# Streaming V as the wide operand of the second-layer attention fill tiles, with the sums picked out of a bf16 high and a bf16 low part

## The chip, the cores and the metric

The kernel runs on one core of a Trainium2 chip. The metric is the device time of one launch in microseconds (us), the median of repeated runs. Three runs of the kernel before gave 316.36, 313.03 and 316.22 us, median 316.22 us.

## The reference

Four decode elements (one query token each, batch B = 4) go through the same two layers twice: grouped-query attention over a cache, then a GEGLU feed-forward block. Both attention passes read the same K and V caches and the same weights.

```python
def _A_ref(x, k_cache, v_cache, wq, wo):          # 32 query heads, 8 KV heads, Sk = 4096, Dh = 128
    q = (x @ wq).reshape(B, 1, 32, 128).transpose(0, 2, 1, 3)
    k = jnp.repeat(k_cache, 4, axis=1)
    v = jnp.repeat(v_cache, 4, axis=1)
    p = softmax(einsum("bhqd,bhkd->bhqk", q, k) * 128 ** -0.5)
    o = einsum("bhqk,bhkd->bhqd", p, v)
    return o.transpose(0, 2, 1, 3).reshape(B, 1, 4096) @ wo
def _B_ref(x, w_gate, w_up, w_down):              # D = 512, F = 1792
    return (gelu(x @ w_gate) * (x @ w_up)) @ w_down
x = x + A(layernorm(x)); x = x + B(layernorm(x))
x = x + A(layernorm(x)); x = x + B(layernorm(x))
```

All inputs are bf16. The K and the V cache have 16.8 million elements each.

## The kernel before, in words

**Tiles.** For one element, K and V are 8 KV heads x 2 halves (`t` = 0, 1) = 16 tiles each of 128 partitions x 16 rows x 128 columns (512 KB). K tiles of one element stay in 16 fixed buffers (`KT`); V tiles go through a ring of 7 buffers (`VRing`, `V_SLOTS = 7`). All DMAs are issued on SyncE (SP) in program order: `Keys.load` (L318) for K, `VRing.pump` (L423) for V. `pump` issues the next V tile of a fixed sequence as soon as a ring buffer is free; a buffer is free when the last matmul that reads it is done.

**Order of the elements.** The order of instructions is written out by hand (`tc.manual_schedule()`); each engine works through its own list in that order. Layer 1 of element b and layer 2 of element b-1 share one load of K and V as far as buffers allow. `attend(b)` first scores layer 2 of element b-1 against the K tiles that are still there (`scores`, L336), and each K tile that is done with is reloaded for element b. Then V arrives: first 16 tiles for layer 1 of b (the last 3 of these are kept in their buffers for layer 2), then 8 tiles, `other2`, which layer 2 of element b-1 needs again, then 5 tiles `own1` for layer 2 of element b. After layer 1's last tile the output projection ends (`OutProj`, L204), and `dense` runs the feed-forward block of element b: `add_x`, `stats`, the gate matmuls `g`, the up matmuls `u`, the down matmuls `y`. Then the main loop (from L714) makes the second layer's query and calls `attend(b+1)`.

**Values.** `Values.step` (L442) takes one V tile: 16 matmuls at L457, each with a 128x128 piece of V as the stationary operand (a weight load) and the 4 probability columns of the head as the moving one, summed into `ot`. When both tiles of two heads are done, VectorE multiplies `ot` by the reciprocal of the softmax sum (L479). `fill(n)` takes n tiles and leaves that multiply for `flush`.

**Where the 8 `other2` tiles stand.** They are filled into the feed-forward block and the query of the next layer, where no other V tile is used, for b = 1, 2 and 3. In the order of TensorE (PE) these places are, with the tiles taken there:

| place | where | before | after |
|---|---|---|---|
| P1 | `dense`, after `add_x`, ahead of `stats` | tile 1 | unit 1 |
| P2 | `dense`, after `g`, ahead of `u` | tile 2 | unit 2 |
| P3 | `dense`, after `u`, ahead of `down` | tile 3 | units 3, 4 |
| P4 | loop, after `add_x`, ahead of `stats` and `q_proj` | tile 4 | unit 5 |
| P5 | loop, after `q_proj`, ahead of `q_build` | tiles 5, 6 | unit 6, turn of pair 1 |
| P6 | loop, after `q_build`, ahead of `attend` | tiles 7, 8 | units 7, 8 |
| P7 | `attend`, after the scores of the first half | - | turn of pair 2 |

Three buffers of the ring hold the kept tiles at this time, so four circulate: tile 5 is issued when tile 1 is done with, and so on; `own1` follows tile 8.

**Softmax.** `soft` (L341 to L360), `soft_turn` (L363) and `soft_swap` (L378) make the probabilities `pe`, 128 partitions x (4 heads x 32 x 4) bf16, by way of PSUM tile `x` (one buffer) and a copy on ScalarE (ACT).

Of the kernel before, what the change touches and what calls it, by code (L numbers as in the profile page):

```python
# [31 lines left out]
def kernel(  # L32
# [35 lines left out]
    wts = ctx.enter_context(tc.tile_pool(name="wts", bufs=1))  # L68
    state = ctx.enter_context(tc.tile_pool(name="state", bufs=1))
    tmpp = ctx.enter_context(tc.tile_pool(name="tmpp", bufs=1))  # L70
    pep = ctx.enter_context(tc.tile_pool(name="pep", bufs=3))
    grp = ctx.enter_context(tc.tile_pool(name="grp", bufs=2))
    zp = ctx.enter_context(tc.tile_pool(name="zp", bufs=2 * NG))
    small = ctx.enter_context(tc.tile_pool(name="small", bufs=1))
# [29 lines left out]
    ident_bf = const.tile([P, P], BF16, name="ident_bf")  # L104
    mean_f = const.tile([P, P], FP32, name="mean_f")
    sel_bf = const.tile([P, BE, QD, QS], BF16, name="sel_bf")
    amask = const.tile([P, QD], FP32, name="amask")
    hmask = const.tile([P, rep], FP32, name="hmask")
    dmask = const.tile([P, GH, rep], FP32, name="dmask")
# [27 lines left out]
    def build_consts():  # L137
        nc.scalar.preload_act_table_set("natural_log_exp_and_others")
        nc.vector.memset(mean_f[:], 1.0 / D)
        nc.vector.memset(qb[:], 0.0)  # L140
        nc.vector.memset(xb[:, :, B:B + 1], 1.0 / D)
        nc.vector.tensor_reduce(out=amask[:], in_=ident_bf[:].rearrange("p (a i) -> p a i", a=QD),
                                axis=AX.X, op=ALU.max)
        iv = ident_bf[:].rearrange("p (b w e) -> p b e w", b=NB, e=2)
        for be in range(BE):
            nc.vector.tensor_copy(out=sel_bf[:, be],
                                  in_=iv[:, be // 2, be % 2].unsqueeze(1)
                                  .broadcast_to([P, QD, QS]))
        nc.vector.tensor_reduce(out=hmask[:], in_=ident_bf[:].rearrange("p (y h) -> p h y", h=rep),
                                axis=AX.X, op=ALU.max)  # L150
        nc.vector.scalar_tensor_tensor(
            out=dmask[:], in0=amask[:].unsqueeze(2).broadcast_to([P, GH, rep]), scalar=float(D),
            in1=hmask[:].unsqueeze(1).broadcast_to([P, GH, rep]), op0=ALU.mult, op1=ALU.mult)
# [12 lines left out]
    def ln_scale(nb, st):  # L166
        ss, mean = st[:, :, 0], st[:, :, 1]
        msq = small.tile([P, nb], FP32, name="msq", tag="msq")
        if nb == 1:
            nc.vector.tensor_scalar(out=msq[:], in0=mean, scalar1=mean, scalar2=LN_EPS,  # L170
                                    op0=ALU.mult, op1=ALU.subtract)
        else:
            nc.vector.tensor_copy(out=msq[:], in_=mean)
            nc.vector.tensor_tensor(out=msq[:], in0=mean, in1=msq[:], op=ALU.mult)
            nc.vector.tensor_scalar(out=msq[:], in0=msq[:], scalar1=LN_EPS, scalar2=None,
                                    op0=ALU.subtract)
        var = small.tile([P, nb], FP32, name="var", tag="var")
# [5 lines left out]
        mr = small.tile([P, nb], FP32, name="mr", tag="mr")  # L183
# [156 lines left out]
    def soft(sc):  # L340
        m = grp.tile([P, 1], FP32, name="m", tag="m", bufs=1)  # L341
        nc.vector.tensor_reduce(out=m[:], in_=sc.rearrange("p c j -> p (c j)"), axis=AX.X,  # L342
                                op=ALU.max)
        mt = grp.tile([P, QS], FP32, name="mt", tag="mt", bufs=1)
        nc.vector.transpose(out=mt[:], in_=m[:].broadcast_to([P, QS]))
        gm = grp.tile([P, rep], FP32, name="gm", tag="gm", bufs=1)
        nc.vector.tensor_reduce(out=gm[:], in_=mt.rearrange("p (y h) -> p h y", h=rep), axis=AX.X,
                                op=ALU.max)
        nm = grp.tile([P, 1], FP32, name="nm", tag="nm")
        junk = grp.tile([P, rep], FP32, name="junk", tag="junk", bufs=1)  # L350
        nc.vector.scalar_tensor_tensor(out=junk[:], in0=gm[:], scalar=-scale, in1=hmask[:],  # L351
                                       op0=ALU.mult, op1=ALU.mult, accum_out=nm[:])
# [20 lines left out]
        nc.vector.reciprocal(out=rden[:], in_=den[:])  # L373
        return rden

    def soft_swap(p0):
        pp = p0[0]
        x = ps_x.tile([P, GH, NT, CH, rep], FP32, name="x", tag="x")  # L378
        pT = pp.rearrange("p c (t a h) -> p a t c h", t=NT, a=QD)
        for s in range(GH):  # L380
            for a in range(QD):
                nc.tensor.matmul(x[a * QS:(a + 1) * QS, s], lhsT=ident_bf[:, s * QS:(s + 1) * QS],  # L382
                                 rhs=pT[:, a], start=True, stop=True, skip_group_check=True)
        pe = pep.tile([P, GH, C, rep], BF16, name="pe", tag="pe")
        nc.scalar.copy(out=pe.rearrange("p s c h -> p (s c h)"),  # L385
                       in_=x.rearrange("p s t c h -> p (s t c h)"))
        return pe
# [96 lines left out]
            return len(self.tiles) - self.n  # L484


    def dst1(k, n):
        return OT_bf[:, k * rep:(k + n) * rep]

# [73 lines left out]
        ring.extend(2, b, own)  # L563
        return proj.y

    def attend(b, qy):

        gx, gy = second_groups[b - 1]
        prob1, prob2 = {}, {}
# [1 line left out]
        turn = keys.turn  # L571
        kept2, own2, other2 = two(b - 1)
        kept1, own1, _ = two(b)
        vals2 = Values(2, b - 1, kept2 + own2 + other2, prob2, dst2(b - 1))
        vals1 = Values(1, b, one(b), prob1, dst1, keeps=kept1)

        sc2 = [new_scores() for g in range(NG)]
        for t in range(NT):
            scores(sc2[0], gx, t)
            keys.load(GH)  # L580
        p0 = soft(sc2[0])
        q_build(qy())
        soft_turn(p0)
# [13 lines left out]
        vals2.step(4)  # L597
        turn()
        vals2.step(3)
        pe1, den1 = soft_swap(p1), soft_den(p1)  # L600
        turn()
        prob2[gy] = (pe1, soft_recip(den1))
        sc1 = new_scores()
# [10 lines left out]
        q_build(q1_bf[:, gy, :, b])  # L614
        turn()
        vals2.step(len(kept2 + own2) - vals2.n)
        vals1.step(2)
        sc1 = new_scores()
        scores(sc1, gy, 0)
# [16 lines left out]
        vals1.step(1)  # L636
        proj.heads(heads[3] + rep, rep)
        assert vals1.left() == 0
        return proj.y, vals2

    def attend_last(qy):
        b = B - 1
        gx, gy = second_groups[b]
        prob2 = {}
        kept2, own2, other2 = two(b)
        vals = Values(2, b, kept2 + own2 + other2, prob2, dst2(b))
        ring.extend(2, b, other2)
        sc2 = [new_scores() for g in range(NG)]
        for t in range(NT):
            scores(sc2[0], gx, t)  # L650
            ring.pump([KT[gx * GH + s][t] for s in range(GH)])
# [10 lines left out]
        prob2[gy] = (soft_swap(p1), soft_recip(soft_den(p1)))  # L662
# [12 lines left out]
        return proj.y  # L675

    def dense(b0, nb, y, prev):
# [18 lines left out]
        prev.fill(1)  # L696
        u = sums(1, ffn_in(rhs, n, wu_sb, "u"))
        H_bf = gate_up(nb, sq, u, shifts(nb, mr, 1), rstd)
        prev.flush()
        prev.fill(1)  # L700
        return down(nb, H_bf)

    class NoValues:
        def fill(self, n):
            pass

        def flush(self):
            pass
# [5 lines left out]
    for b in range(B):  # L714
# [11 lines left out]
        nc.vector.tensor_scalar(out=tq[:], in0=cs_q[:], scalar1=mr[:, 0:1], scalar2=None,  # L726
                                op0=ALU.mult)
        qx = q_round(q, gx, rstd, tq)
        prev.flush()
        prev.fill(2)  # L730
        q_build(qx)
        prev.flush()
        prev.fill(TG)
        prev.flush()

        def qy(b=b, g=gy, rstd=rstd, tq=tq):
            return q_round(q_proj(lambda k: xb[:, k, b:b + 1], 1, g), g, rstd, tq)

        if b < B - 1:
            y, prev = attend(b + 1, qy)  # L740
        else:
            y = attend_last(qy)

    add_x(0, B, dense(0, B, y, NoValues()))
    xo_ps = ps_sm.tile([P, D], BF16, name="xo_ps", tag="sm")
# [35 lines left out]
```

## Time and profile before

| | |
|---|---|
| median of 3 runs | 316.22 us (313.03 to 316.36) |
| the profiled execution's own time | 315.57 us |
| its span, first to last instruction | 313.8 us |
| outside the span | 1.8 us |
| PE busy | 208.7 us, 66%, 5104 matmuls |
| DVE (VectorE) / ACT busy | 145.1 us, 46% / 32.9 us, 10% |
| DMA | 106.90 MB, mean 341 GB/s |
| chain that ended last | DMA 56%, PE 26%, DVE 7% |

The span is cut from the first to the last instruction of the program. PE is matmuls, PEld the weight loads that run beside them. In a timeline line the columns are start, duration, engine, source line, operation, out<-in by the program's names, shape, and the count of merged instructions; in brackets stands the idle time before the first of them and what ended it ("issue" means that the profile shows nothing that the engine waited for). "SPq" is SyncE's DMA queue. In the chain the columns are start, duration and what it was.

### The profile page before, as it was taken

What the parts mean: (1) busy time and instruction counts of PE and PEld (TensorE: products, weight loads), DVE (VectorE), ACT (ScalarE), POOL (GpSimd) and SP (SyncE); (2) the same over time, 40 slices, a digit from 0 to 9 for tenths busy, and PEclk for the clock granted to TensorE, in tenths of its full rate; (3) what the DMA queues carried; (4) which work ended last, traced back from release to release, by engine and by line L of the source; (5) the groups of instructions that cost most, each with busy time, mean ns of one, the idle gap of its engine ahead of it and who ended that gap; (6) DMA issues with size and microseconds to landing.
All of it is one profiled execution on the core that took longest, in us unless ns stands there. A gap on an engine that the chain in (4) does not pass through costs nothing.

```text
span 313.8 us, 11113 instructions
## 1 busy us (share of the span) xinstructions
PE 208.7 (66%) x5104; PEld 153.9 (49%) x5104; DVE 145.1 (46%) x372; ACT 32.9 (10%) x90; POOL 0.7 (0%) x6
## 2 busy tenths in 40 slices
PE   1464275324787667887838387788583778878893
PEld 0213145324546145786425247685261468845893
DVE  3576812012267894032378961322689731313333
ACT  2002002000012112000110202000022020002200
POOL 0000000000000000000000000000000000000000
PEclk9999999999999999999875655555557555555555
DMA  7999999999179999978999999968999999779800
GB/s 255 384 417 421 421 416 395 376 407 399 34 263 401 417 419 418 415 290 239 350 418 416 421 386 344 364 218 260 413 416 421 415 418 392 240 256 359 321 7 3
DMA packets 33503, 106.90 MB, mean 341 GB/s; under 512 B 2984, under 2 KB 8880, under 8 KB 33456
## 3 DMA queue, kind: packets, MB, share of 16 engines
q1 hardware_dynamic: 33456, 106.19, 88.3%
q8 instruction: 40, 0.66, 0.8%
q14 instruction: 7, 0.06, 0.1%
HBM read 106.17 MB, written 0.00 MB: 338 GB/s over the span
## 4 chain that ended last, share of the span: by engine, by line
DMA 56%; PE 26%; DVE 7%; SPq 5%; issue 4%; ACT 2%; ACTq 0%
DMA v_t<-in_A_v_cache_dram 27%; DMA kt<-in_A_k_cache_dram 23%; PE sc L336 7%; PE ot L457 6%; DMA wd_sb<-in_B_w_down_dram 5%; PE y L204 5%; PE q L204 2%; SPq L130 2%; ACT pp L355 2%; PE g L204 1%; PE u L204 1%; DVE m L342 1%; PE x L382 1%; SPq L131 1%; DVE pp L363 1%
## 5 line engine op out<-in xcount | busy, mean ns | idle before, releaser
L457 PE MATMUL ot<-pe,v_t 128*128 128x4 bf16 x1904 | 62.5, 167 | 29.0 <-DMA v_t<-in_A_v_cache_dram 19.9
L325 DVE STREAM_TRANSPOSE kt<-kt 128x1024 f32<-128x1024 f32 x64 | 75.1, 1214 | 6.5 <-DMA kt<-in_A_k_cache_dram 6.3
L457 PEld LDWEIGHTS <-v_t 128*128 128x128 bf16 x1904 | 58.5, 105 | 39.0 <-DMA v_t<-in_A_v_cache_dram 22.4
L336 PE MATMUL sc<-kt,qb 128*32 128x512 bf16 x512 | 62.9, 608 | 10.3 <-DVE kt L325 7.8
L336 PEld LDWEIGHTS <-qb 128*32 128x32 bf16 x512 | 17.3, 128 | 39.8 <-issue 32.1
L479 DVE TENSOR_TENSOR OT_bf<-ot,rden 128x8 bf16<-128x8 f32 (+1 forms) x40 | 6.5, 163 | 52.2 <-PE ot L457 52.1
L204 PE MATMUL y<-OT_bf,wo_sb 128*128 128x1 bf16 (+1 forms) x640 | 20.5, 165 | 9.4 <-DMA wo_sb<-in_A_wo_dram 7.7
L355 ACT ACTIVATE pp<-sc,nm 128x512 bf16<-128x512 f32 x16 | 11.0, 687 | 148.7 <-DVE junk L351 148.7
L204 PEld LDWEIGHTS <-wo_sb 128*128 128x128 bf16 x640 | 19.8, 105 | 10.0 <-DMA wo_sb<-in_A_wo_dram 8.1
L204 PE MATMUL q<-xb,wq_sb 128*128 128x1 bf16 (+1 forms) x640 | 18.5, 165 | 7.2 <-DMA wq_sb<-in_A_wq_dram 7.2
L204 PEld LDWEIGHTS <-wq_sb 128*128 128x128 bf16 x640 | 17.8, 103 | 11.2 <-DMA wq_sb<-in_A_wq_dram 8.2
L342 DVE TENSOR_REDUCE m<-sc 128x1 f32<-128x512 f32 x16 | 10.9, 682 | 25.2 <-PE sc L336 25.1
L382 PE MATMUL x<-pp,ident_bf 128*32 128x128 bf16 x256 | 9.7, 297 | 17.3 <-DVE pp L363 17.3
L382 PEld LDWEIGHTS <-ident_bf 128*32 128x32 bf16 x256 | 6.5, 124 | 19.9 <-issue 19.3
L368 PE MATMUL den<-zx,mean_f 128*128 128x16 f32 x32 | 9.7, 382 | 8.9 <-DVE qb L225 8.9
L368 PEld LDWEIGHTS den<-zx,mean_f 128*128 128x128 f32 x32 | 8.0, 312 | 12.1 <-issue 12.1
L249 DVE TENSOR_TENSOR xb<-XX,y 128x4 bf16<-128x4 f32 (+1 forms) x10 | 1.7, 171 | 25.0 <-PE y L204 25.0
L385 ACT CAST pe<-x 128x512 bf16<-128x512 f32 x16 | 9.3, 582 | 28.2 <-PE x L382 28.2
L363 DVE STREAM_TRANSPOSE pp<-pp 128x512 bf16<-128x512 bf16 x16 | 11.1, 692 | 2.0 <-ACT pp L355 2.0
L204 PE MATMUL y<-H_bf,wd_sb 128*128 128x1 bf16 (+1 forms) x280 | 8.8, 166 | 4.6 <-DVE H_bf L291 2.8
L204 PE MATMUL g<-xb,wg_sb 128*128 128x1 bf16 (+2 forms) x280 | 8.3, 165 | 4.1 <-DMA wg_sb<-in_B_w_gate_dram 3.0
L180 ACT ACTIVATE var<-var 128x1 f32<-128x1 f32 (+1 forms) x10 | 2.0, 203 | 83.9 <-DVE var L178 83.9
(68 smaller groups left out, 116.2 us busy)
## 6 DMA issues: line engine op xcount, KB each, us to landing
v_t<-in_A_v_cache_dram SPq DMA_DIRECT2D x103, 512.0 KB, 8.1
kt<-in_A_k_cache_dram SPq DMA_DIRECT2D x64, 512.0 KB, 10.0
kt<-in_A_v_cache_dram SPq DMA_DIRECT2D x9, 512.0 KB, 11.0
wq_sb<-in_A_wq_dram SPq DMA_DIRECT2D x2, 2048.0 KB, 11.2
wo_sb<-in_A_wo_dram SPq DMA_DIRECT2D x4, 1024.0 KB, 11.0
wg_sb<-in_B_w_gate_dram SPq DMA_DIRECT2D x1, 1792.0 KB, 12.8
wu_sb<-in_B_w_up_dram SPq DMA_DIRECT2D x1, 1792.0 KB
wd_sb<-in_B_w_down_dram SPq DMA_DIRECT2D x2, 896.0 KB, 15.6
```

What stands on the lines that cost most here:

```text
L130: dq.dma_start(out=wo_sb[:, i * n:(i + 1) * n], in_=wo_dram[:, i * n:(i + 1) * n])
L204: nc.tensor.matmul(dst, lhsT=lhsT, rhs=rhs, start=first, stop=last, skip_group_check=True)
L325: nc.vector.transpose(out=words, in_=words)
L336: nc.tensor.matmul(sc[s * QS:(s + 1) * QS], lhsT=qb[:, w0:w0 + 2 * W], rhs=kt[:, :, be // 2, :, be % 2], start=(t == 0 and be == 0), stop= ...
L342: nc.vector.tensor_reduce(out=m[:], in_=sc.rearrange("p c j -> p (c j)"), axis=AX.X, op=ALU.max)
L355: nc.scalar.activation(out=pp[:], in_=sc[:], func=ACT.Exp, bias=nm[:, 0:1], scale=scale, accum_out=ls[:])
L363: nc.vector.transpose(out=flat, in_=flat)
L368: nc.tensor.matmul(den[:], lhsT=mean_f[:, :], rhs=zx[:], start=True, stop=True)
L382: nc.tensor.matmul(x[a * QS:(a + 1) * QS, s], lhsT=ident_bf[:, s * QS:(s + 1) * QS], rhs=pT[:, a], start=True, stop=True, skip_group_check ...
L385: nc.scalar.copy(out=pe.rearrange("p s c h -> p (s c h)"), in_=x.rearrange("p s t c h -> p (s t c h)"))
L457: nc.tensor.matmul(self.ot[:, s % 2], lhsT=v[:, i, :], rhs=pe[:, s, t * CH + i, :], start=(done == 0 and i == 0), stop=(done == NT - 1 and ...
L479: nc.vector.tensor_tensor(out=self.dst(unit[0], n).rearrange("p (k h) -> p k h", h=rep), in0=ot[:, s % 2:s % 2 + n], in1=rden[:, s:s + n], ...
```

## The change

`other2` is reordered to go by pairs of heads and, within a pair, by half `t`: (h0,0), (h1,0), (h0,1), (h1,1). The class `Streamed` takes the place of `Values` for these 8 tiles of b = 1, 2, 3 (`Values` keeps the kept and own ones, all of layer 1, and all of the last element). A unit is half of two tiles: four matmuls, each with 32 probability columns (8 rows of the cache x 4 heads) as the stationary operand and 512 columns of V (4 rows x 128) as the moving one. The four write different 32-partition groups of one PSUM tile `so`. A unit uses both tiles of its half; the first unit of a half waits for both tiles, the second frees both. After four units (one pair of heads) ACT copies `so` to bf16 (`hi`), VectorE subtracts that from `so` (`lo`, bf16), and 8 matmuls (`turn`) with 128x128 pieces of `hi` and `lo` as stationary operand and a 0/1 matrix `pick` as the moving one add up the wanted blocks into `ot`; the multiply by the reciprocal follows. `so` uses the one PSUM buffer of `x`; `hi` and `lo` use the buffers of `pe`, which go from 3 to 2 beside a new single buffer `pl` for the probabilities that outlive `attend`. Small buffers `mr` and `junk` are merged with others.

```diff
-    pep = ctx.enter_context(tc.tile_pool(name="pep", bufs=3))
+    pep = ctx.enter_context(tc.tile_pool(name="pep", bufs=2))
...
+        iv = ident_bf[:].rearrange("p (i z c h) -> p c i z h", i=2, z=16 // QD, h=rep)
+        nc.vector.tensor_tensor(out=pick[:], in0=iv[:, :, :, 0], in1=iv[:, :, :, 3], op=ALU.add)
...
+    class Streamed:
...
+        def fill(self, count):
+            for _ in range(count):
+                if self.n == 4 * len(self.pairs):
+                    return
+                (p, u), self.n = divmod(self.n, 4), self.n + 1
+                t, half = divmod(u, 2)
+                pair = self.pairs[p]
+                g, s = divmod(pair[0], GH)
+                pe = self.prob[g][0]
+                if u == 0:
+                    self.ps = ps_x.tile([P, QD * Dh], FP32, name="so", tag="x")
+                if half == 0:
+                    ring.pump()
+                    self.v = [ring.ready.pop((2, self.b, h, t))[0] for h in pair]
+                w = t * CH + 2 * QD * half
+                for i in range(2):
+                    for z in range(2):
+                        j, c = 2 * i + z, 2 * QD * half + QD * z
+                        nc.tensor.matmul(self.ps[j * QS:(j + 1) * QS],
+                                         lhsT=pe[:, s + i, w:w + 2 * QD].rearrange("p c h -> p (c h)"),
+                                         rhs=self.v[i][:, c:c + QD].rearrange("p c d -> p (c d)"),
+                                         start=u == 0, stop=u == 3)
+                if half == 1:
+                    ring.free += self.v
+                    ring.pump()
+                if u == 3:
+                    hi = pep.tile([P, QD * Dh], BF16, name="hi", tag="pe")
+                    nc.scalar.copy(out=hi[:], in_=self.ps[:])
+                    self.done.append((pair, self.ps, hi))
+
+        def low(self):
+            pair, ps, hi = self.done.pop()
+            lo = pep.tile([P, QD * Dh], BF16, name="lo", tag="pe")
+            nc.vector.tensor_tensor(out=lo[:], in0=ps[:], in1=hi[:], op=ALU.subtract)
+            self.done.append((pair, hi, lo))
+
+        def turn(self):
+            pair, hi, lo = self.done.pop()
+            g, s = divmod(pair[0], GH)
+            ot = ps_ot.tile([P, 2, rep], FP32, name="ot", tag="ot")
+            for x in (hi, lo):
+                for c in range(QD):
+                    nc.tensor.matmul(ot.rearrange("p i h -> p (i h)"), lhsT=x[:, c * Dh:(c + 1) * Dh],
+                                     rhs=pick[:, c].rearrange("p i h -> p (i h)"),
+                                     start=x is hi and c == 0, stop=x is lo and c == QD - 1)
+            nc.vector.tensor_tensor(
+                out=self.dst(pair[0], 2).rearrange("p (k h) -> p k h", h=rep),
+                in0=ot[:], in1=self.prob[g][1][:, s:s + 2], op=ALU.mult)
...
-        vals2 = Values(2, b - 1, kept2 + own2 + other2, prob2, dst2(b - 1))
+        duos = [(other2[i][0], other2[i + NT][0]) for i in range(0, len(other2), 2 * NT)]
+        other2 = [(h, t) for duo in duos for t in range(NT) for h in duo]
+        vals2 = Values(2, b - 1, kept2 + own2, prob2, dst2(b - 1))
+        late2 = Streamed(b - 1, duos, prob2, dst2(b - 1))
...
             scores(sc2[0], gx, t)
             keys.load(GH)
+            if t == 0:
+                prev.turn()
...
         H_bf = gate_up(nb, sq, u, shifts(nb, mr, 1), rstd)
-        prev.flush()
-        prev.fill(1)
+        prev.fill(2)
+        prev.low()
         return down(nb, H_bf)
...
         qx = q_round(q, gx, rstd, tq)
-        prev.flush()
+        prev.fill(1)
+        prev.turn()
+        q_build(qx)
         prev.fill(2)
-        q_build(qx)
-        prev.flush()
-        prev.fill(TG)
-        prev.flush()
+        prev.low()
```

More of the change, by code (lines that the diff above doesn't have):

```diff
@@ L106 @@
     sel_bf = const.tile([P, BE, QD, QS], BF16, name="sel_bf")
+    pick = const.tile([P, QD, 2, rep], BF16, name="pick")
     amask = const.tile([P, QD], FP32, name="amask")
@@ L182, in ln_scale @@
         nc.scalar.activation(out=rstd[:], in_=var[:], func=ACT.Exp, scale=-0.5)
-        mr = small.tile([P, nb], FP32, name="mr", tag="mr")
+        mr = small.tile([P, nb], FP32, name="mr", tag="msq")
         nc.vector.scalar_tensor_tensor(out=mr[:], in0=mean, scalar=float(D), in1=rstd[:],
@@ L349, in soft @@
         nm = grp.tile([P, 1], FP32, name="nm", tag="nm")
-        junk = grp.tile([P, rep], FP32, name="junk", tag="junk", bufs=1)
-        nc.vector.scalar_tensor_tensor(out=junk[:], in0=gm[:], scalar=-scale, in1=hmask[:],
+        nc.vector.scalar_tensor_tensor(out=gm[:], in0=gm[:], scalar=-scale, in1=hmask[:],
                                        op0=ALU.mult, op1=ALU.mult, accum_out=nm[:])
@@ L374, in soft_recip, with soft_swap @@
         return rden
-    def soft_swap(p0):
+    def soft_swap(p0, lasting=False):
         pp = p0[0]
@@ L383, in soft_swap @@
                                  rhs=pT[:, a], start=True, stop=True, skip_group_check=True)
-        pe = pep.tile([P, GH, C, rep], BF16, name="pe", tag="pe")
+        pe = (pep.tile([P, GH, C, rep], BF16, name="pl", tag="pl", bufs=1) if lasting else
+              pep.tile([P, GH, C, rep], BF16, name="pe", tag="pe"))
         nc.scalar.copy(out=pe.rearrange("p s c h -> p (s c h)"),
@@ L484, in left, with __init__ @@
             return len(self.tiles) - self.n
+    class Streamed:
+        def __init__(self, b, pairs, prob, dst):
+            self.b, self.pairs, self.prob, self.dst, self.n = b, pairs, prob, dst, 0
+            self.v, self.done = [], []
+        def fill(self, count):
[44 more added lines that the diff above has]
+                in0=ot[:], in1=self.prob[g][1][:, s:s + 2], op=ALU.mult)
@@ L564, in attend_first, with attend @@
         return proj.y
-    def attend(b, qy):
+    def attend(b, qy, prev):
         gx, gy = second_groups[b - 1]
@@ L599, in attend @@
         vals2.step(3)
-        pe1, den1 = soft_swap(p1), soft_den(p1)
+        pe1, den1 = soft_swap(p1, lasting=True), soft_den(p1)
         turn()
@@ L616, in attend @@
         vals2.step(len(kept2 + own2) - vals2.n)
+        assert vals2.left() == 0
         vals1.step(2)
@@ L638, in attend, with attend_last @@
         assert vals1.left() == 0
-        return proj.y, vals2
-    def attend_last(qy):
+        return proj.y, late2
+    def attend_last(qy, prev):
         b = B - 1
@@ L650, in attend_last @@
             scores(sc2[0], gx, t)
+            if t == 0:
+                prev.turn()
             ring.pump([KT[gx * GH + s][t] for s in range(GH)])
@@ L661, in attend_last @@
         soft_turn(p1)
-        prob2[gy] = (soft_swap(p1), soft_recip(soft_den(p1)))
+        prob2[gy] = (soft_swap(p1, lasting=True), soft_recip(soft_den(p1)))
         vals.step(2)
@@ L705, in fill @@
             pass
-        def flush(self):
-            pass
+        low = turn = lambda self: None
     x_bf = tmpp.tile([P, D], BF16, name="x_bf", tag="pp")
@@ L728 @@
         qx = q_round(q, gx, rstd, tq)
-        prev.flush()
+        prev.fill(1)
+        prev.turn()
+        q_build(qx)
         prev.fill(2)
-        q_build(qx)
-        prev.flush()
-        prev.fill(TG)
-        prev.flush()
+        prev.low()
         def qy(b=b, g=gy, rstd=rstd, tq=tq):
@@ L739 @@
         if b < B - 1:
-            y, prev = attend(b + 1, qy)
+            y, prev = attend(b + 1, qy, prev)
         else:
-            y = attend_last(qy)
+            y = attend_last(qy, prev)
     add_x(0, B, dense(0, B, y, NoValues()))
```

## The prediction

> **What bounds the kernel now.** I read the chain that ended last first: DMA 56% and PE 26%. The DMA rate in the page's slices stands near 420 GB/s with dips around 80, 140, 205 and 275 us. The last three are the feed-forward blocks of elements 1 to 3, the only place that the change touches. There the chain in order of time runs:
>
> ```profile
> 142.30 5.09 DMA v_t<-in_A_v_cache_dram
> 147.39 0.05 issue
> 147.43 0.59 PE ot L457 x16
> 148.02 1.93 PE sc L336 x15
> 149.95 0.24 SPq L318
> ...
> 150.29 9.34 DMA kt<-in_A_k_cache_dram
> ```
>
> The eighth fill tile, then the scores, then the K reloads: what moves the start of the scores (147.95, 213.66, 278.89 us) moves the rest. So I walk the timeline of PE from the end of the output projection to the scores (13.45, 13.35, 14.1 us for elements 1, 2, 3). Its lines for element 1:
>
> ```profile
> 134.50 0.57 PE L457 MATMUL ot<-pe,v_t 128*128 128x4 bf16 x16
> 134.93 0.25 PE L161 MATMUL st<-xb 128*128 128x2 bf16 x4
> 135.04 1.63 PE L204 MATMUL g<-xb,wg_sb 128*128 128x1 bf16 x56
> 136.53 0.38 PE L457 MATMUL ot<-pe,v_t 128*128 128x4 bf16 x9
> 137.76 0.34 PE L457 MATMUL ot<-pe,v_t 128*128 128x4 bf16 x7 [0.85 <-issue]
> 137.97 1.63 PE L204 MATMUL u<-xb,wu_sb 128*128 128x1 bf16 x56
> ...
> 146.59 0.56 PE L457 MATMUL ot<-pe,v_t 128*128 128x4 bf16 x15 [1.52 <-issue]
> 147.43 0.59 PE L457 MATMUL ot<-pe,v_t 128*128 128x4 bf16 x16 [0.29 <-DMA v_t<-in_A_v_cache_dram]
> ```
>
> Two things are to be seen. From start to start a tile of 16 matmuls takes 134.93 - 134.50 = 0.43 us, 27 ns a pair of weight load and matmul. And PE pauses in the middle of a tile, with nothing that it waits for. Between the pauses before 132.94 and 137.76 lie 128 pairs. The page has
>
> ```profile
> q8 instruction: 40, 0.66, 0.8%
> ```
>
> that is 40 blocks of 16.5 KB for PE's 10,208 matmuls and loads, 128 pairs a block. I read these pauses as waits for the next block of instructions (inferred). They are 0.85 + 1.52 = 2.4 us in element 1, 1.24 + 0.18 + 1.00 = 2.4 in element 2, 1.06 + 0.16 + 2.08 = 3.3 in element 3: 8.1 us, by far the largest waste in these windows.
>
> **What a unit costs.** The nearest rows are the scores (L336, also 32 stationary and 512 moving columns into four groups) and the swap (L382, 128 moving columns):
>
> ```profile
> 86.77 0.15 PEld L336 LDWEIGHTS <-qb 128*32 128x32 bf16 x4 [0.28 <-issue]
> 87.19 0.15 PEld L336 LDWEIGHTS <-qb 128*32 128x32 bf16 x4 [0.28 <-issue]
> 88.18 1.78 PEld L204 LDWEIGHTS <-wq_sb 128*128 128x128 bf16 x64 [0.84 <-issue]
> ```
>
> ```profile
> 157.62 0.41 PE L382 MATMUL x<-pp,ident_bf 128*32 128x128 bf16 x16
> 293.11 0.62 PE L382 MATMUL x<-pp,ident_bf 128*32 128x128 bf16 x16 [0.29 <-DVE pp L363]
> ```
>
> Four scores matmuls follow the last four by 0.43 us. The swap's 16 took 0.62 us where the granted clock was 0.50 and 0.41 us where it was 1.00; in elements 2 and 3 the clock in the windows is 0.50. So a unit streams for 0.43 us at half clock; half of that, 0.22, is my estimate for the full clock and the lower end. I take 0.43, the scores' row: no gain over the 0.43 of a tile. There is a border besides: the scores begin 0.10 us after the last V matmul instead of 0.03 (0.07), and after 8 groups x 0.43 = 3.41 us from 84.65 the next full-width matmul starts at 88.19, 0.13 late. A single unit costs 0.63 us, a double 1.06, and the double ahead of the scores 0.93 (same shape behind it).
>
> [...]
>
> **The steps, element by element.** Removed: 128 pairs. Added: 32 streaming matmuls in 8 units, 16 pairs for the two turns. New waits: P1 needs tiles 1 and 2 instead of 1; P4 needs tiles 5 and 6, which are issued only when P2 has freed two buffers (before, tile 5 was issued after P1 and needed at P5). Landings: tile 2 of element 1 was issued at 128.47 and took 6.5 us, so 134.97; of element 2 at 194.51 with 7.4, so 201.95; of element 3 at 259.42 with 6.5, so 265.92. A pair issued into a nearly empty queue is not in the trace for this place; a single tile took 4.1 to 5.3 us there, the second of two K tiles at 87.02 5.2 us, and of two V tiles behind one that was still under way 7.0 (issued at 212.57) to 7.4 us (144.96). I take 5.2, the emptiest queue, and keep 7.0 for the range.
>
> Element 1: P1 waits to 135.02, ends 135.58. `stats` and `g` 1.60: 137.18. P2 0.63: 137.81; tiles 5 and 6 issue at 137.9 and 138.35. `u` 1.49: 139.30. P3 1.06: 140.36 (it hides the 0.24 us wait for H_bf at 139.9). `down` 1.56: 141.92. P4: tile 6 is there at 143.55, a wait of 1.6; unit to 144.1. `stats` and `q` 1.81: 145.9. P5 0.63, turn 8 x 0.027 = 0.25 with its start: 146.8; `q_build` 0.11: 146.9. P6 0.93: 147.85. Scores at 147.85 against 147.95: -0.1. Behind the waiting unit at P4 stand `stats` and the whole query, so nothing hides that wait.
>
> Element 2, same steps from P1 at 202.0: scores at 214.85 against 213.66, +1.2. Element 3 from 265.97: 278.8 against 278.89, -0.1. Sum +1.0, with every pause gone.
>
> Pauses: 372 pairs in 13.4 us become some 290 matmuls in the same time, so a block lasts 5.9 us instead of 4.6, and much of that is waiting, in which the next block comes. Ends: 0 and the 2.4 us of before. I take 0.3 each, as the blocks are then longer than the 4 to 5 us from one pause's end to the next's: +0.9.
>
> Turn of pair 2 (P7): 8 pairs and two borders, 0.42 us. The last element's tail is PE from the scores on, so all of it counts; in the other two the second K group waits for its queue anyway (0 to 0.42, I take 0.15): +0.7. If `lo` came late, the second scores would wait behind the turn: `hi` costs 0.58 us (L385), `lo` 0.69 (L342's row), under the first scores' 1.7 us. The same pair after P3 is covered by `down` (1.56). DVE's add_x queues behind `lo` there, with 0.2 us to spare.
>
> K's queue: own1's first two tiles are issued 1.2 us ahead of the scores instead of 3.4 (144.54), so a little work is pushed behind: 0 to 0.6 for two elements, I take 0.2 each: +0.4. `pick` is one small DVE operation at about 2.4 us, while the first K is on its way until 11.98; `mr` and `gm` stay on DVE in order: nothing.
>
> Sum: 1.0 + 0.9 + 0.7 + 0.4 = +3.0 on the profiled execution's 315.57 us (313.8 and 1.8 outside): **318.6 us**. That execution lies 0.65 us under the median shown, so against 316.22 this is +0.75%. One per cent, 3.2 us, is about what a measurement of this kernel can tell from no change.
>
> **Rivals.**
> Slower: the pair lands late. At P4 the second tile takes 7.0 us instead of 5.2: +1.8 x 3 = +5.4, 324.0 us. It decides as soon as the pair takes over 5.5 us. For it: 7.0 and 7.4 us in two rows. Against: those had another tile ahead.
> Faster: the clock. 24 units at 0.22 instead of 0.43 save 5.0 us, and no pause is left (-0.9): 312.7 us. For it: the clock did go to 1.00 in four short stretches, one after scores. Against: 0.50 over both later windows.
> No effect: the train of K loads takes up the shift of elements 1 and 2 (its landings from 147.39 to 160.9 are further apart than in the full queue), and only the last turn and a pause count: +0.5, 316 us.
>
> **How the numbers follow.** Forecast 0.54 (315.5 to 321.5, a third of it above 319.4), slower rival 0.22, faster 0.14, no effect 0.10. Slower by over 1%: 0.22 + 0.18 = 0.40; faster 0.14; within 1% 0.46. The range goes from the faster rival's 312.7 to the slower one's 324.0.
>
> **What the profile after would show.** Few "issue" pauses in the three windows; waits for V at P1 (0.5, 1.6, 1.0 us) and P4 (1.6 us) instead; units 0.43 us apart; scores within 1.5 us of their old place. I am wrong if the pauses stay, if the units run at 0.22, or if the wait at P4 is 0 or over 3 us.

## The result and the profile after

| | before | after |
|---|---|---|
| median, us | 316.25 (313.03 to 316.36) | 323.92 (323.46 to 324.87) |
| the profiled execution's own time, us | 315.57 | 323.51 |
| its span, us | 313.8 | 321.7 |
| PE busy, us | 208.7 (5104 matmuls) | 214.6 (4864 matmuls) |
| ACT busy, us | 32.9 | 36.4 |
| DMA | 106.90 MB, 341 GB/s | 106.87 MB, 332 GB/s |

The ratio after to before is 1.027, with a 95% interval of 1.020 to 1.034. (Medians here and below are over all runs; ratios leave out the runs that took over 1.5% longer than the fastest of the same kernel.) The forecast was +0.75%. The sign is right; most of the loss was not in the forecast.

The prediction walked through three windows, from PE's first fill tile to the first scores, since nothing else was to change. So I cut both spans there (each is one profiled execution):

| us | before | after | difference |
|---|---|---|---|
| start to window 1 | 134.50 | 138.55 | +4.05 |
| window 1 | 13.45 | 13.47 | +0.02 |
| to window 2 | 52.36 | 53.46 | +1.10 |
| window 2 | 13.35 | 14.20 | +0.85 |
| to window 3 | 51.13 | 52.69 | +1.56 |
| window 3 | 14.10 | 14.37 | +0.27 |
| to the end | 34.91 | 34.96 | +0.05 |
| the windows together | 40.90 | 42.04 | +1.14 |
| the rest together | 272.90 | 279.66 | +6.76 |

The windows, where the change's code runs, lost 1.14 us. Everything else lost 6.76 us, and 4.05 of it before a single streamed unit had run. That is where to look next, and the rate of the transfers shows it. In stretches without a window, where the DMA engines are always busy (a share of 1.03), the answer for before reads as follows (stretch; its length; busy time of PE, its weight loads, VectorE, ScalarE, GpSimd; granted clock; share of the DMA engines; GB/s):

```profile
110.00:125.00 15.00, 10.42 (x215) 6.83 (x214) 10.70 (x19) 2.07 (x7) 0.00 (x0) 1.00 1.03 420
165.00:185.00 20.00, 13.42 (x260) 8.34 (x257) 17.84 (x25) 2.26 (x5) 0.00 (x0) 0.59 1.03 418
230.00:250.00 20.00, 13.19 (x252) 8.11 (x250) 17.83 (x25) 2.26 (x5) 0.00 (x0) 0.59 1.03 417
```

The same stretches of after, moved by its delay:

```profile
114.00:129.00 15.00, 10.81 (x218) 7.14 (x211) 9.66 (x17) 2.06 (x5) 0.00 (x0) 1.00 1.03 409
170.00:190.00 20.00, 11.98 (x207) 6.91 (x205) 17.38 (x25) 2.26 (x5) 0.00 (x0) 0.59 1.03 408
237.00:257.00 20.00, 12.29 (x189) 6.53 (x187) 17.20 (x25) 2.25 (x5) 0.00 (x0) 0.50 1.02 408
```

The DMA engines are as fully busy as before (1.02 to 1.03) and move 2.4% less (on average 408 GB/s against 418). The trace's packet records say the same: a packet of 1024 bytes (the rows of `wo` and `w_down`) takes 46.5 ns on average before and 50.6 after, one of 3584 bytes (`w_gate` and `w_up`) 140.5 and 145.9, one of 4096 bytes (K and V, in these stretches) 159.5 and 163.1. Before, nearly all packets of 1024 bytes (99%) take 46 ns; after, a third do, and the rest spread up to 60.

What in the change could slow transfers before a single streamed unit runs? `pick`. It is 64 bytes per partition in the pool `const`, and that pool lies ahead of every weight, K and V buffer. In the built program `wq` moves from byte 18432 of a partition to 18496, the first K buffer from 126976 to 127040, the first V buffer from 192512 to 192576: from multiples of 512 to 64 past one. The experiments test this first.

Inside the windows the forecast's picture holds. The chain that ended last, its longest pieces in order of time, around window 1 of after (start, duration, what):

```profile
142.34 5.38 DMA v_t<-in_A_v_cache_dram
147.77 0.61 PE so L515 x2
148.59 1.71 PE q L207 x64
150.29 0.55 PE so L515 x4
150.84 0.31 PE ot L539 x8
151.26 0.97 PE so L515 x8
152.24 1.71 PE sc L339 x14
153.94 0.32 PE ot L539 x8
154.38 8.86 DMA kt<-in_A_k_cache_dram
```

The second tile of the pair for P4 lands 5.38 us after its issue, and P4, the query, the turn and the scores stand in line behind it. The turn of pair 2 (153.94) is on the chain too. The timeline of PE shows the wait at P4:

```profile
143.40 1.05 PE L515 MATMUL so<-v_t,pl 128*32 128x512 bf16 x8
144.38 1.65 PE L207 MATMUL y<-H_bf,wd_sb 128*128 128x1 bf16 x56
146.51 0.61 PE L515 MATMUL so<-v_t,pl 128*32 128x512 bf16 x2 [0.48 <-DMA v_t<-in_A_v_cache_dram]
147.77 0.61 PE L515 MATMUL so<-v_t,pl 128*32 128x512 bf16 x2 [0.65 <-DMA v_t<-in_A_v_cache_dram]
148.31 0.27 PE L164 MATMUL st<-xb 128*128 128x2 bf16 x4
148.45 1.85 PE L207 MATMUL q<-xb,wq_sb 128*128 128x1 bf16 x64
150.22 0.62 PE L515 MATMUL so<-v_t,pl 128*32 128x512 bf16 x4
150.78 0.27 PE L539 MATMUL ot<-pick,hi 128*128 128x8 bf16 x4
```

The idle times in brackets, 0.48 and 0.65 us, are not all that the wait costs. The two matmuls on the first tile keep PE "busy" while the second tile is on its way, but they save nothing: the two on the second tile take 0.54 us to the start of what follows (147.77 to 148.31), and a whole unit of four takes 0.56 (150.22 to 150.78). So below I also count the delay: from the place where the unit could have begun, 1.58 us behind the start of `down` where nothing is waited for, to the matmuls on the second tile. Here that is 147.77 - 145.96 = 1.81 us.

And the pauses that nothing explains, 8.1 us in the three windows before, are one of 0.60 us in element 2. The instruction queue's line in the page of after:

```profile
q8 instruction: 38, 0.62, 0.8%
```

### The profile page after: what moved, and what is told of

The parts are those of the page before. It is cut to its first block, busy times and chain, and to the rows that moved or that the text cites. A ratio compares the mean times of both kernels' runs of the same rounds, so it can differ in the third digit from the quotient of the medians.

```text
span 321.7 us, 10656 instructions
## 1 busy us (share of the span) xinstructions
PE 214.6 (67%) x4864; PEld 147.8 (46%) x4864; DVE 149.7 (47%) x379; ACT 36.4 (11%) x96; POOL 0.7 (0%) x6
## 2 busy tenths in 40 slices
DMA packets 33501, 106.87 MB, mean 332 GB/s; under 512 B 2984, under 2 KB 8880, under 8 KB 33456
## 3 DMA queue, kind: packets, MB, share of 16 engines
q1 hardware_dynamic: 33456, 106.19, 86.9%
## 4 chain that ended last, share of the span: by engine, by line
DMA 58%; PE 25%; DVE 6%; SPq 5%; ACT 2%; issue 2%; ACTq 0%
DMA v_t<-in_A_v_cache_dram 30%; DMA kt<-in_A_k_cache_dram 23%; PE sc L339 6%; DMA wd_sb<-in_B_w_down_dram 5%; PE ot L460 5%; PE so L515 3%; PE y L207 3%; PE q L207 3%; SPq L131 2%; ACT pp L357 1%; PE g L207 1%; DVE m L345 1%; SPq L132 1%; PE x L384 1%; DVE pp L365 1%
## 5 line engine op out<-in xcount | busy, mean ns | idle before, releaser
L328 DVE STREAM_TRANSPOSE kt<-kt 128x1024 f32<-128x1024 f32 x64 | 75.4, 1215 | 5.5 <-DMA kt<-in_A_k_cache_dram 5.4
L460 PE MATMUL ot<-pe,v_t 128*128 128x4 bf16 x1520 | 48.7, 167 | 25.3 <-DMA v_t<-in_A_v_cache_dram 22.8
L460 PEld LDWEIGHTS <-v_t 128*128 128x128 bf16 x1520 | 46.2, 105 | 34.8 <-DMA v_t<-in_A_v_cache_dram 25.3
L482 DVE TENSOR_TENSOR OT_bf<-ot,rden 128x8 bf16<-128x8 f32 (+1 forms) x34 | 5.5, 163 | 53.3 <-PE ot L460 53.3
L515 PE MATMUL so<-v_t,pl 128*32 128x512 bf16 x96 | 17.6, 612 | 4.0 <-DMA v_t<-in_A_v_cache_dram 3.9
L370 PEld LDWEIGHTS den<-zx,mean_f 128*128 128x128 f32 x32 | 8.0, 312 | 11.2 <-issue 11.2
L207 PEld LDWEIGHTS <-wd_sb 128*128 128x128 bf16 x280 | 7.9, 104 | 6.9 <-DVE H_bf L294 4.3
```

The costliest lines, as they stand in the source:

```text
L207: nc.tensor.matmul(dst, lhsT=lhsT, rhs=rhs, start=first, stop=last, skip_group_check=True)
L328: nc.vector.transpose(out=words, in_=words)
L370: nc.tensor.matmul(den[:], lhsT=mean_f[:, :], rhs=zx[:], start=True, stop=True)
L460: nc.tensor.matmul(self.ot[:, s % 2], lhsT=v[:, i, :], rhs=pe[:, s, t * CH + i, :], start=(done == 0 and i == 0), stop=(done == NT - 1 and ...
L482: nc.vector.tensor_tensor(out=self.dst(unit[0], n).rearrange("p (k h) -> p k h", h=rep), in0=ot[:, s % 2:s % 2 + n], in1=rden[:, s:s + n], ...
L515: nc.tensor.matmul(self.ps[j * QS:(j + 1) * QS], lhsT=pe[:, s + i, w:w + 2 * QD].rearrange("p c h -> p (c h)"), rhs=self.v[i][:, c:c + QD] ...
```

## The experiments

Each comparison measured the kernel before again beside the others, so its median differs a little: 315.28, 316.06 and 315.70 us. Two theories stood at the start. **Layout**: the 64 bytes move the DMA buffers and that alone slows every transfer. **Waits**: the loss comes from the pairs (P1, P4), and the rest follows from a queue that runs empty at the wrong time.

### The layout alone, without the change

```diff
 # the kernel before
+    pad = const.tile([P, 32], BF16, name="pad")
...
+        nc.vector.memset(pad[:], 0.0)
```

> The kernel before with one unused 64-byte constant ahead of the weights, so that every DMA destination (weights, K, V) starts 64 bytes past a multiple of 512, as in the changed kernel; no other work changes. Theory A (the place of the buffers slows the DMAs): 1024-byte packets rise from 46 to about 50 ns, 4096-byte ones from 159 to about 163, the rate in the full stretches falls from about 418 to 408 GB/s, and the time is about 321.5 us (5.4 us of the 7.9 that the changed kernel lost lie outside the three windows). Theory B (that difference is the chip of that day or comes with the streamed units): 316 us, packets as before.

Measured: 321.07 us against 315.28, ratio 1.018 (1.011 to 1.025). The full stretches:

```profile
113.00:128.00 15.00, 9.89 (x198) 6.42 (x198) 10.24 (x18) 1.69 (x5) 0.00 (x0) 0.50 1.02 409
168.00:188.00 20.00, 12.66 (x219) 7.25 (x216) 17.11 (x24) 2.26 (x5) 0.00 (x0) 0.50 1.03 410
235.00:255.00 20.00, 12.65 (x246) 7.86 (x244) 17.79 (x24) 2.26 (x5) 0.00 (x0) 0.59 1.03 408
```

The rate of after, with no line of the change but an unused buffer. Window 1 begins at 138.68 us, +4.18, as in after (+4.05). The packets of 1024, 3584 and 4096 bytes take 50.7, 146.0 and 162.9 ns. VectorE's transposes of K and PE's matmuls on V, which read the same moved buffers, keep their durations (1214 ns in the kernel before and 1215 here; 167 and 166): of the three, only the transfers became slower.

### The change without the layout

```diff
 # the changed kernel
-    pick = const.tile([P, QD, 2, rep], BF16, name="pick")
+    pick = small.tile([P, QD, 2, rep], BF16, name="pick", tag="pick")
```

> The changed kernel with the 64 bytes of pick moved behind all DMA destinations, which then lie as in the kernel before. Theory A: packets and rate as before, time 318 to 319 us: only the three windows' +0.4, +1.3 and +0.7 us are left. Theory B: 324 us.

Measured: 320.64 us, ratio 1.017 (1.012 to 1.022). The pool `small` lies behind the buffers, so they are back at multiples of 512, and the rate with them (in the first stretch 417 GB/s here and 409 in the run before stand beside the same granted clock of 0.50, so the clock is not what sets it):

```profile
112.00:127.00 15.00, 10.61 (x219) 7.13 (x220) 9.29 (x18) 2.15 (x5) 0.00 (x0) 0.50 1.03 417
167.00:187.00 20.00, 13.39 (x230) 7.64 (x228) 17.86 (x26) 2.26 (x5) 0.00 (x0) 0.50 1.03 417
233.00:253.00 20.00, 13.45 (x239) 7.77 (x237) 17.70 (x25) 2.26 (x5) 0.00 (x0) 0.50 1.03 419
```

So the layout explains part of the loss and not all. Cut as above, this kernel loses 3.5 us in the windows (14.26 + 14.73 + 15.43 = 44.42 against 40.90) and 1.9 outside, where after lost 6.8.

### Which start is good enough

All DMA buffers at an odd multiple of 256 (the identity moved out of `const` too):

```diff
 # the changed kernel with pick in small
-    ident_bf = const.tile([P, P], BF16, name="ident_bf")
+    ident_bf = small.tile([P, P], BF16, name="ident_bf", tag="ident_bf")
```

> The changed kernel with pick and the identity moved behind all DMA destinations, which then start at a multiple of 256 but not of 512 bytes. If 256 is what matters: as the run with 512, 318 to 319 us and 159 ns packets. If 512 is: slower packets and about 321 to 324 us. [...]

All DMA buffers at an odd multiple of 128, without the change (packets as with 64, or as with 256?):

```diff
 # the kernel before; dmask and hmask likewise
-    amask = const.tile([P, QD], FP32, name="amask")
+    amask = small.tile([P, QD], FP32, name="amask", tag="amask")
```

> The kernel before with the three small masks `amask`, `hmask`, `dmask` (128 bytes) moved from the constants ahead of the DMA buffers to the pool behind them: all DMA buffers start 128 bytes lower, at an odd multiple of 128. [...] Theory `64 or 128` (only a start off a smaller multiple costs): as before, 315 to 317 us, with 46 and 159 ns.

Measured: 320.09 us with 256, ratio 1.016 (1.011 to 1.021), the same as with 512, and packets as in the kernel before (46.4, 140.6, 159.7 ns). With 128, 319.66 us against 315.70, ratio 1.017 (1.012 to 1.021), above the 315 to 317 of theory `64 or 128`, and the packets of the 64-byte shift (50.4, 145.6, 163.0 ns). The rate in full stretches with 128:

```profile
112.00:127.00 15.00, 9.88 (x198) 6.41 (x198) 10.00 (x18) 1.45 (x4) 0.00 (x0) 0.50 1.03 409
167.00:187.00 20.00, 12.97 (x222) 7.33 (x219) 17.34 (x24) 2.25 (x5) 0.00 (x0) 0.50 1.02 407
233.00:253.00 20.00, 13.97 (x252) 8.29 (x252) 17.20 (x26) 2.28 (x6) 0.00 (x0) 0.50 1.03 410
```

Of the four starts tried, 0 and 256 past a multiple of 512 are fast and 64 and 128 past a multiple of 256 are slow, by nearly the same amount per packet (3.9, 5.1 and 3.5 ns with 128). That amount hardly depends on the size: 4.1 ns for 1024 bytes, 5.4 for 3584 and 3.6 for 4096 with 64 bytes. So it is paid per packet and hardly by the byte; why a packet takes longer is not shown by these runs.

### What the rest is: the wait at P4

In the aligned version PE stood idle for V at P4 for 1.62, 1.01 and 2.47 us in the three windows (5.1 together); the delay, counted as above, was 2.30, 1.70 and 3.16 (7.2). Two kernels tell that wait from the cost of changing the shape of the matmuls ("borders" in the expectations). Both have one border less per window; only the first lets the next pair be issued earlier.

```diff
 # the changed kernel with pick in small: P1 takes both units of the first half, P2 none
-        prev.fill(1)
+        prev.fill(2)
         st = stats(b0, nb)
...
-        prev.fill(1)
         u = sums(1, ffn_in(rhs, n, wu_sb, "u"))
```

> The aligned changed kernel (320.6 us), but both units of the first half stand at P1 and none at P2. The pair's buffers come free ahead of `u` and some 2 us of `g` earlier, so the next pair is issued about 2 us earlier. Theory `wait`: the wait at P4 (1.44 to 2.5 us in each of three windows of the aligned version) goes; 314.5 to 316.5 us. Theory `borders` (what the regrouping saves is that units stand next to each other and change the shape of the matmuls less often): one border of 0.20 us less in each window, 320 us.

```diff
 # the changed kernel with pick in small: P4 takes units 5 and 6, P5 only the turn
-        prev.fill(1)
+        prev.fill(2)
         st = stats(b, 1)
...
-        prev.fill(1)
         prev.turn()
```

> The aligned changed kernel (320.6 us), but units 5 and 6 both stand at P4 and only the turn at P5. One border less in each window, as in the kernel with the double P1, but the pair is issued no earlier. Theory `wait`: the wait at P4 stays; 319.5 to 320.6 us. Theory `borders`: as much as the double P1 gives, whatever that is.

Measured, against 316.06: 315.70 us with the double P1, ratio 0.999 (0.995 to 1.004); 320.08 with the double P4, ratio 1.014 (0.998 to 1.029). The timelines of PE around P4 in element 3. First the aligned version:

```profile
275.56 1.65 PE L207 MATMUL y<-H_bf,wd_sb 128*128 128x1 bf16 x56
279.07 0.61 PE L515 MATMUL so<-v_t,pl 128*32 128x512 bf16 x2 [1.85 <-DMA v_t<-in_A_v_cache_dram]
280.30 0.61 PE L515 MATMUL so<-v_t,pl 128*32 128x512 bf16 x2 [0.62 <-DMA v_t<-in_A_v_cache_dram]
```

Then the double P1:

```profile
272.80 1.65 PE L207 MATMUL y<-H_bf,wd_sb 128*128 128x1 bf16 x56
274.38 0.81 PE L515 MATMUL so<-v_t,pl 128*32 128x512 bf16 x4
275.13 0.27 PE L164 MATMUL st<-xb 128*128 128x2 bf16 x4
```

And the double P4:

```profile
275.86 1.65 PE L207 MATMUL y<-H_bf,wd_sb 128*128 128x1 bf16 x56
277.92 0.61 PE L515 MATMUL so<-v_t,pl 128*32 128x512 bf16 x2 [0.41 <-DVE XX L257]
280.17 1.04 PE L515 MATMUL so<-v_t,pl 128*32 128x512 bf16 x6 [1.64 <-DMA v_t<-in_A_v_cache_dram]
```

With both units at P1 the pair of `t` = 0 is done with ahead of `g`; the next pair is issued 1.6 to 3.0 us earlier in the window (its second tile at 2.33, 2.22 and 1.76 us from the window's start instead of 3.92, 5.17 and 4.42) and lands under `down`, and the profile shows no idle time at P4 in any of the three windows (the delay is 0.2 us in window 3 and under 0.1 in the others). It isn't that the pair comes faster: the second tile takes 5.65 us in element 1 and 5.97 in element 2. The windows come to 12.82 + 14.44 + 12.39 = 39.65 us, 4.8 less than in the aligned version, and the medians differ by 4.9. That is a balance: some 6.9 us of delay at P4 and 0.4 of borders are gone, while pauses (2.1 instead of 0.5) and waits at P6 (0.55 in two windows) have come. The double P4 saves a border as well, but its delay at P4 is 2.79, 2.44 and 2.73 us, and its four runs (318.1 to 321.6) lie above nine of the ten of the double P1 (313.5 to 316.7). So it is the early issue of the pair that brings the aligned version back to a tie, and the wait at P4 is the main part of the rest of the loss (each window is read from one execution).

### Is it the grouping or the streaming?

The double P1 ties with the kernel before, though it has no wait at P4 and few pauses. Would grouping alone do as much?

```diff
 # the kernel before: two tiles each at P1, P3, P4, P6, none at P2 and P5
-        prev.fill(1)
+        prev.fill(2)
         st = stats(b0, nb)
...
-        prev.fill(1)
         u = sums(1, ffn_in(rhs, n, wu_sb, "u"))
...
```

> The kernel before, with its 8 fill tiles at the places where the fast streamed version has its units: two at P1, P3, P4 and P6, none at P2 and P5; nothing is streamed. Theory `fetch`: what the streamed version gains over the kernel before are the pauses of PE that nothing explains in the trace (8.1 us in all in the kernel before), which go with the smaller number of PE instructions; grouping alone leaves them, 315 to 317 us. Rival `grouping`: the places alone give the gain, 313 to 314.5 us.

Measured: 315.85 us, ratio 1.001 (0.995 to 1.006): grouping gives the kernel before nothing. Its timeline of PE in window 3 still has the pauses:

```profile
266.12 0.99 PE L204 MATMUL g<-xb,wg_sb 128*128 128x1 bf16 x32
268.07 0.80 PE L204 MATMUL g<-xb,wg_sb 128*128 128x1 bf16 x24 [0.96 <-issue]
...
273.17 1.23 PE L204 MATMUL y<-H_bf,wd_sb 128*128 128x1 bf16 x40 [1.39 <-issue]
...
277.72 0.48 PE L204 MATMUL q<-xb,wq_sb 128*128 128x1 bf16 x12 [0.98 <-issue]
```

In the three windows they come to 7.9 us, against 8.1 before and 0.60 in after; in the streamed kernel with the double P1 they are 2.1 us, all in element 2. Over all runs the four kernels without streaming have 7.6 to 8.1 us, the nine profiles with it 0 to 2.4.

The traces say more on what the pauses are than the prediction's count of blocks did. In all 13 profiles there are 85 pauses over 0.15 us in which PE waits for nothing that the profile shows, and two things hold for each. It lies a multiple of 256 PE instructions (matmuls and weight loads) behind the first one of its profile, to within four; regrouping moves a pause to other work, not to another count. And it ends 1.1 to 1.6 us after a packet of 16,384 bytes on `q8`, the instruction queue, has ended: before, the packet ends at 136.32 and the pause at 137.76, then 145.24 and 146.59. So the prediction's reading as waits for the next block, of 256 instructions, is well supported. At 27 ns a pair such a block is 3.5 us of work. The windows before have 372 pairs each, those of after 284 matmuls with their loads in 13.5 to 14.4 us, so that a block lasts over 6 us there and the next one mostly comes in time; this last step is argued from these numbers, not tested.

### The best version, with and without the layout

Double P1 and double P4 together, aligned, measured twice (the label that ends in "again" is the same kernel):

```diff
 # the changed kernel with pick in small: P1 and P4 take two units, P2 none, P5 only the turn
-        prev.fill(1)
+        prev.fill(2)
         st = stats(b0, nb)
...
-        prev.fill(1)
+        prev.fill(2)
         st = stats(b, 1)
...
```

> The one before, with the units grouped otherwise: two units at P1 (both halves, so tiles 1 and 2 are free 1.5 us earlier), none at P2, two at P4, none at P5. If the waits at P4 and the borders between shapes are what the windows cost: per element two single units at 0.63 us become 0.43 us more in a double (-0.4 us) and the wait at P4 (about 1.6 us) is gone, -1.9 us each, 313 us in all. Rival: the wait only moves, because the pair lands 5.4 us after its issue and P4 then comes 5.5 us after it, or pauses for instructions come back: 317 us or more.

> The regrouped, aligned streamed version once more, on another chip: 0.3 to 1.1% below the kernel before if its gain is real, some 313 to 315 us. If it was a matter of that chip, within 0.3% of it.

And the same kernel with `pick` among the constants:

```diff
-    pick = small.tile([P, QD, 2, rep], BF16, name="pick", tag="pick")
+    pick = const.tile([P, QD, 2, rep], BF16, name="pick")
```

> The fast regrouped version (314.1 us) with `pick` back among the constants, as the changed kernel has it. If layout and grouping are two separate costs, it pays the layout's whole price of 4 to 6 us over the regrouped version on the same chip: 318 to 320 us. If slower transfers only fill the waits at P4, and so cost less where those are gone or more where they stay, the price differs from the 3 to 6 us between the changed kernel and its aligned version.

Measured: 314.09 us against 315.28, ratio 0.993 (0.989 to 0.998), the first time; 315.84 against 315.70, ratio 0.999 (0.995 to 1.003), the second. The gain of the first comparison did not come back, so streaming, done well, is not shown to be faster than the kernel before. With `pick` among the constants the same kernel takes 321.47 us in the second comparison, ratio 1.021 (1.016 to 1.027), 5.6 us more for 64 bytes: the layout costs as much where the wait at P4 is gone.

The changed kernel itself, once more:

> The changed kernel unchanged, beside the other three on the same chip. If the 64 bytes of `pick` ahead of the DMA buffers cost time on any chip, it is again 2.2 to 3.2% above the kernel before (322 to 326 us against some 315.5 to 316). If the first comparison was a matter of that chip, it lands at the 1.7% of the aligned version, some 321 us.

Measured: 326.25 us against 316.06, ratio 1.035 (1.026 to 1.045), somewhat above what was expected.

## Why the prediction was wrong in size

**The step that failed** is the one that priced `pick`: "`pick` is one small DVE operation at about 2.4 us, while the first K is on its way until 11.98 ...: nothing." It priced the operation that fills the buffer and not the buffer's place, and put the term at 0. Measured, in differences of medians:

| comparison | us |
|---|---|
| kernel before, 64 bytes added | +5.8 |
| kernel before, DMA buffers 128 bytes lower | +4.0 |
| best streamed version, 64 bytes added | +5.6 |
| changed kernel against its aligned version, by the medians | +3.3 |
| the same by the ratios of the second measurement (1.0352 - 1.0171) x 316 | +5.7 |

A sum that can be made once the rates are measured: 106.19 MB (`q1` on the page) at 418 GB/s are 254.0 us, at 409 GB/s 259.6, so +5.6 us if the queue never ran dry. Had the forecast had 4.0 to 5.8 us here, it would have read 322.6 to 324.4.

**What held.** The chain and its bottleneck were read rightly; the windows' own cost was forecast as 1.0 + 0.9 = +1.9 us and came to +1.14, and to +3.0 in the second profile of the changed kernel. Term by term, forecast and after (first profile):

- A unit: 0.63 us alone, 1.06 doubled, 0.93 doubled ahead of the scores; measured from start to start 0.55, 0.98 and 0.83 (141.26 to 141.81, 143.40 to 144.38, 151.19 to 152.02). The 0.43 us of the scores' row was right and the borders were a little too dear. No unit ran at 0.22. The granted clock has to be read with care here: it shows 1.00 at the scores' row at 86.77 us and in window 1, where scores and units are as slow as where it shows 0.50, but the trace records its first change of clock only at 150.78 us before and 154.48 after. In a short stretch behind that with 1.00 (171.8 us, before) the scores did run 0.22 to 0.23 us apart. So 0.22 was a fair estimate for such a stretch, but the windows' units ran at the pace seen with 0.50.
- The landing of the pair: 5.2; measured 5.38, 5.01 and about 5.55 (from the start of the matmuls; that landing is not recorded). The wait at P4: 1.6 in each window, counted to the second tile; as a delay counted in the same way it was 1.81, 1.44 and 1.98 (idle time 1.13, 0.64 and 1.29). At P1: 0.5, 1.6 and 1.0; the delay was 0.47, 0.84 and 1.22 (idle time shown 0, 0.23 and 0.61). Both terms were about right.
- Pauses: 0.9 left of 8.1; measured 0.60.
- The turn of pair 2: 0.42 where it counts; on the chain it is 0.31 to 0.32. `hi` took 0.58 us and `lo` 0.69, as forecast, under the first scores and under `down`.
- The turns and K's queue outside the windows: 0.7 + 0.4. In the aligned version the rest lost 1.9 us, but 1.2 of it ahead of window 1, where no streamed unit has run; these terms can't be told from the spread.

**The rivals.** The slower rival named 324.0 us, and the median is 323.92. That is a coincidence: its mechanism, a pair that takes 7.0 us, isn't in the trace of after. It does come part of the way in the aligned version, where the awaited second tile took 6.05 us in element 1 and some 6.7 in element 3, and the windows lost 3.5 us instead of 1.9. So the forecast without the failed step, +0.75%, would have been low for that kernel too (+1.7%), and the term that was too small there is the wait at P4: a delay of 7.2 us in all where the prediction had 4.8.

**Layout and wait apart.** By the medians, 5.8 for the shift alone and 5.4 for the aligned change would add up to 11.2, where the changed kernel lost 7.7 and, measured again, 10.2. Cutting every profile at the windows shows where each part lies (us more than the 40.9 and 272.9 of the kernel before; the column of starts has multiples of 512, 64 past them, and odd multiples of 128 and 256):

| kernel | DMA rows start at | windows | the rest |
|---|---|---|---|
| before, 64 bytes added | 512 + 64 | +0.1 | +6.3 |
| before, 128 bytes lower | odd 128 | -0.7 | +4.8 |
| changed, first profile | 512 + 64 | +1.1 | +6.8 |
| changed, second profile | 512 + 64 | +3.0 | +7.8 |
| best streamed, `pick` in `const` | 512 + 64 | -1.7 | +6.2 |
| changed, aligned | 512 | +3.5 | +1.9 |
| changed, aligned to 256 | odd 256 | +2.8 | +1.5 |
| double P4, aligned | 512 | +4.5 | +1.6 |
| double P1, aligned | 512 | -1.3 | +1.8 |
| best streamed, first profile | 512 | -2.5 | +0.1 |
| best streamed, second profile | 512 | -0.3 | +2.3 |
| before, regrouped | 512 | +2.1 | -1.0 |

The layout is paid outside the windows (4.8 to 7.8 us where it is shifted, -1.0 to 2.3 where it is not), whatever stands inside them; the wait at P4 is paid inside. Each row is one execution, and executions of one kernel differ by 2 us and more (the kernel before took 313.03 to 316.36 us).

**What stays open** is why the pair lands earlier in one execution than in another. The changed kernel's delay at P4, all windows together, is 5.2 us in its first profile and 6.5 in its second; the aligned versions' is 7.2 and, with 256, 6.2. So the smaller loss of the first profile is not shown to come from the layout.

## What to carry to other kernels

A new constant is also a new layout: look up where it pushes the buffers that DMAs write to, and measure the packets there. Here it helped to put it behind them (ratio 1.017 instead of 1.027 and 1.035), and starts at odd multiples of 256 bytes did as well (1.016); 64 bytes ahead of the buffers cost as much (5.6 to 5.8 us) as the whole mistake in the order of the work (4.9 to 5.4). When a kernel loses time before the changed code first runs, compare the transfer rate in full stretches ahead of anything else. And when two tiles are used together, free the previous two together and early: here the place from which the next pair could be issued decided (double P1), and the place where it was used did not (double P4). Last, an idle time in a profile can be less than the delay (1.13 us of idle time at P4 in window 1, 1.81 of delay): look at when the work behind it starts.

## What the runs showed of the hardware that was not expected

- The start of a row in SBUF set how fast these DMAs wrote it: 46.5 ns for 1024 bytes, 140.5 for 3584 and 159.5 for 4096 where it lies at a multiple of 256, and 50.6, 145.9 and 163.1 at an offset of 64; 128 is like 64 (50.4, 145.6 and 163.0). In every kernel of this study the full stretches show 417 to 420 GB/s with the one and 407 to 410 with the other.
- PE's unexplained pauses stand at multiples of 256 PE instructions and end 1.1 to 1.6 us after a 16 KB packet of the instruction queue, in all 85 cases. They went from 8.1 to 0.60 us in the windows when 128 pairs of load and matmul became 32 wide matmuls and 16 pairs. That gain went into the new waits, borders and turns: the streamed version without the two defects ties with the kernel before (ratio 0.999).
- Two of a unit's four 32-column matmuls took as long as all four: 0.54 and 0.56 us to the start of what follows.
